# A fused attention and two expert layers: order of the pooled products, one more early place for a weight tile, an even schedule of weight loads

## The chip, the cores and the metric

The kernel runs on one core of one Trainium2 chip, in one launch. The metric is the device time of that launch in microseconds. The core's engines are named as in the profile: PE is TensorE's matmul stream and PEld its loads of the stationary operand, DVE is VectorE, ACT ScalarE, POOL GpSimd, and SP the engine whose queue issues all DMA transfers here.

## The reference

Three stages, all in 32-bit floats. The first is attention over 4 batches, 8 heads, 576 positions and head size 64. It has two branches. The pooled branch averages q, k and v over groups of four positions (144 of them), does full softmax attention and repeats each output row four times. The local branch lets each position see only neighbours at a distance under four:

```
q_d, k_d, v_d = mean over groups of 4;  out_up = repeat(sm_attn(q_d, k_d, v_d), 4)
scores = where(|i - j| < 4, scale * q @ k.T, -1e9)
out = out_up + softmax(scores) @ v          # then (B, H, S, D) -> x of (2304, 512)
```

The second stage is a soft mixture of experts: `logits = x @ phi` (32 slots), a softmax over tokens makes 32 slot inputs, each of 8 experts takes four of them through `relu(s @ w1) @ w2` (512 to 1024 to 512), and a softmax over slots gives each token its mixture. The third is a second mixture with 8 experts over all 2304 tokens, whose gates are normalised eight times over rows and columns in turn; the result is the sum of `P[:, e] * relu(x @ w1[e]) @ w2[e]`.

## The kernel before, in words

**Units and steps.** The attention is cut into 16 units: one batch and one pair of heads each, with the 2 x 64 head columns on 128 partitions. The work on a unit is some 35 small parts (`load_q`, `transpose_k`, `score_pool`, `pool_exp`, `av_pool`, `x_add` and so on, functions of the unit's number). A list written out by hand, `ORDER`, names the parts with a lag; step u of the loop calls part p for unit u - lag. So at any time parts of about seven units are in flight, and every engine executes its instructions in the order in which the list emits them. Step u loads q for unit u + 3 and k for unit u + 4, transposes q of unit u + 2, and does the pooled and local products of unit u - 2. Parts in `BATCH` run once in four steps (the logits of the expert layer and their running softmax). What is left of units 14 and 15 and of the last batch stands in a second list, `TAIL`, with some idle matmuls (`tail_fill`).

**The parts around the change.** `pt` (L549, L554) transposes the normalised pooled probabilities and pools v; `pt_copy` (L562, L566) copies both out of PSUM as `ptd` and `vd`. `av_pool` (L578) multiplies them into `up`: for each of the two heads one product over 128 rows of that head's own block and one over 64 rows of the block that the two heads share, accumulated into that head's 64 output partitions. Before, the order is own and shared of head 0, then own and shared of head 1. In the trace each fp32 matmul is two matmul and two weight-load instructions. `up_copy` (L587) copies `up` to `ups`, of which there are two buffers; `av_loc` (L595) makes the local output `loc`, twelve matmuls with the heads in turn; `x_add` (L605) adds `ups`, repeated four times, to `loc` and writes one of five tiles `xt0` to `xt4` (unit modulo 5). `x_nat` (L628, L629) transposes `xt` for the token layout. `score_pool` (L458) makes the pooled scores `sd` of the next unit in one PSUM buffer, which `pool_exp` (L501) reads.

**Weights of the first expert layer.** Both weight matrices are read as 32 tiles `wa` of 128 x 2048 floats, 8,192 bytes a partition and 1024 KB each (`load_wa`, L311), in the order of `wa_order`. The first 20 have places of their own: `NW` = 4, then `NX` = 7, 4 and 5. The 4 + 7 = 11 exist from the start, on the left of SBUF below the attention's pools. The next 4 lie on the right, where q, k and their transposes were, and exist after the last `score_pool`. The last 5 lie on the left over the attention's pools `ld` (three buffers vw), `st` (two block diagonals), `wk` (work tiles) and `wl` (`xt0` to `xt4` and small ones), in that order of addresses, and are asked for when `TAIL` has been emitted; two further tiles ("late") follow above them. Tiles 23 to 32 reuse the first places as the layer's first products `h` (L877) free them. Loads wait place by place: a tile's transfer waits for the last reader of whatever lies under it, and since one queue issues them, a load behind a waiting one waits too.

`LOADS` says at which step how many weight tiles are asked for (`load_w`); a load of a step stands on SP behind q and k of that step and ahead of v. After the last step all places that exist are filled.

**The first expert layer after the attention.** `h` takes the sixteen tiles of w1, expert by expert (the last two are the late ones, the 21st and 22nd tile), then `so` (L934) the sixteen tiles of w2. Then the second layer begins (`ap`, L992), whose weights w1s and w2s come on the same queue and whose order is planned by due times; the change leaves it alone.

Of the kernel before, what the change touches and what calls it, by code (L numbers as in the profile page):

```python
# [8 lines left out]
FP32 = mybir.dt.float32  # L9
# [31 lines left out]
    ("tail_fill", 2), ("tok_sum", 3), ("tail_fill", 5), ("tok_add", 3),  # L41
]

LOADS = {-2: 1, 2: 1, 4: 1, 6: 1, 8: 1, 10: 1, 12: 1, 13: 1, 14: 1, 15: 2}

PADDED = 2

# [138 lines left out]
def attn_moe_moe_kernel(  # L186
# [23 lines left out]
    SD = S // 4  # L210
# [1 line left out]
    NSET = S // (4 * QB)  # L212

    QS = 1.0 / float(D) ** 0.5 / 16.0
    NW, NX = 4, (7, 4, 5)
    BLK = 256
    NB = N // BLK

# [64 lines left out]
    def load_next(n=1):  # L283
        nonlocal nw
        for _ in range(n):
            if nw < 4 * E:
                load_wa(nw)
                nw += 1
# [29 lines left out]
    with ExitStack() as actx:  # L318
# [5 lines left out]
        wk = actx.enter_context(tc.tile_pool(name="wk", bufs=2))  # L324
# [245 lines left out]
        def av_pool(u):  # L570
            d = U[u]
            up = d["up"] = p1.tile([128, SD], FP32, name="up", tag="t1")
            vd, ptd = d["vd"], d["ptd"]
            for h in range(2):

                for i in (2 * h, 1):
                    ks = slice(64 * h, 64 * h + 64) if i == 1 else slice(0, 128)
                    nc.tensor.matmul(  # L578
                        out=up[64 * h:64 * h + 64, :], lhsT=vd[ks, i, :], rhs=ptd[ks, i, :],
                        start=(i != 1), stop=(i == 1),  # L580
                    )

        def up_copy(u):
            d = U[u]
            up = d["up"]
            ups = d["ups"] = wk.tile([128, 2, SD // 2, 1], FP32, name="ups", tag="ups")
            nc.scalar.activation(out=ups, in_=up.rearrange("p (a g o) -> p a g o", a=2, o=1), func=ACTF.Copy)  # L587

        def av_loc(u):
# [211 lines left out]
        for u in range(-3, nu):  # L801
            for n, lag in ORDER:
                if n == "load_w":
                    load_next(LOADS.get(u, 0))
                elif n not in BATCH:
# [29 lines left out]
    with mctx:  # L835
# [18 lines left out]
        for j in range(KD):  # L854
            nc.tensor.matmul(
                out=sit[:, j].rearrange("p e s -> p (e s)"), lhsT=ssum[:, 128 * j:128 * j + 128], rhs=stack[:, 0, :],
                start=True, stop=True,
# [13 lines left out]
        for e in range(E):  # L871
# [4 lines left out]
            for a, j in order:  # L876
# [3 lines left out]
                    start=(e == 0), stop=(e == E - 1),  # L880
# [36 lines left out]
        for j in range(KF):  # L917
# [3 lines left out]
                start=True, stop=True,  # L921
# [4 lines left out]
        for e in range(E):  # L926
            for j in range(KF):
                g = j % 4
                w = wt[2 * E + 2 * e + j // 4]
                if e >= E - 2 and j % 4 == 0:  # L930
# [5 lines left out]
                    start=(e == 0 and j < 4), stop=(e == E - 1 and j >= 4),  # L936
# [492 lines left out]
```

## Time and profile before

| what | us |
|---|---|
| median of 3 runs (lowest, highest) | 1014.33 (1012.17, 1015.3) |
| profiled execution, its own time | 1014.82 |
| its span, first to last instruction | 1013.1 |
| PE / PEld busy | 979.1 / 900.4 |
| DVE / ACT / POOL busy | 713.5 / 550.6 / 592.9 |

The mean granted clock of TensorE in that execution is 0.997 of 2.4 GHz. The chain of work that ended last has 84% of its time on PE, 5% on ACT, 4% on DVE and 3% on DMA. The 40 slices of the page show DMA busy at 0.9 or more of the time in the first 100 us, about 0.6 to 0.8 in the next 50, again 0.9 in the 50 after that, and little later. Stretches of the span: steps of the attention to about 135 us, `TAIL` to about 163, `h` to 180, `so` to 207, then the second expert layer.

A line of the timeline reads: start, duration, engine, line, operation, out<-in, shape and count, and in brackets the engine's idle time before it with what ended it. A line of the chain reads: start, duration, what the end of the program was waiting for at that time. In the stretches, each engine has its busy time and number of instructions; then follow TensorE's granted clock, the busy share of the DMA engines (over 1 where transfers overlap) and GB/s.

### The profile page before, as it was taken

The page shows a single profiled execution, that of the slowest core. Times are in us where ns is not written, and L with a number is a line of the kernel's source. Part 1 is how long each engine was busy: PE and PEld are TensorE (multiplying, and loading weights), DVE is VectorE, ACT ScalarE, POOL GpSimd, SP SyncE. Part 2 cuts the span into 40 slices and gives each one's busy share as a digit, 9 for nine tenths or more (in the row PEclk, how much of TensorE's full clock was granted, in tenths as well). Part 3 has the DMA queues.
Part 4 walks back from the last instruction along what each step waited for, and adds up shares of the span by engine and source line. Part 5 has one row for each costly group of instructions (what it writes and reads, how often), then busy time and mean ns, then how long its engine had stood idle before and what let it go on. Part 6 is the DMA issues. An engine that isn't in the chain of part 4 may idle for free.

```text
span 1013.1 us, 23034 instructions
## 1 busy us (share of the span) xinstructions
PE 979.1 (97%) x9353; PEld 900.4 (89%) x9353; DVE 713.5 (70%) x1251; ACT 550.6 (54%) x1055; POOL 592.9 (59%) x456
## 2 busy tenths in 40 slices
PE   5999999889999999999999999999999999999998
PEld 4776665469999899989999999999999999999998
DVE  5878862255887767767686768667866776778766
ACT  4666641154566656745565556455655555565453
POOL 6554431033667557855774676576757674776544
PEclk9999999999999999999999999999999999999999
DMA  9999688944002200220031004000400130000111
GB/s 186 211 179 214 166 302 306 387 182 167 1 2 84 84 1 2 87 81 1 2 125 43 1 2 163 5 2 8 160 1 2 42 126 2 2 2 21 64 43 63
DMA packets 96956, 89.11 MB, mean 88 GB/s; under 512 B 65876, under 2 KB 65876, under 8 KB 96852
## 3 DMA queue, kind: packets, MB, share of 16 engines
q1 hardware_dynamic: 96852, 87.65, 29.4%
q8 instruction: 74, 1.21, 0.5%
q14 instruction: 30, 0.25, 0.1%
HBM read 82.92 MB, written 4.72 MB: 87 GB/s over the span
## 4 chain that ended last, share of the span: by engine, by line
PE 84%; ACT 5%; DVE 4%; DMA 3%; issue 2%; POOL 1%; SPq 1%; ACTq 0%; DVEq 0%; POOLq 0%
PE y L1121 63%; PE z L1063 6%; DMA wa<-in_moe_w_dram 3%; PE up L578 2%; PE y L1134 2%; PE ap L992 2%; DVE wt L1053 2%; ACT pd L501 1%; ACT kt L412 1%; PE sd L458 1%; PE knt L368 1%; PE as L1003 1%; DVE acc L1159 1%; PE loc L595 1%; PE sl L445 1%
## 5 line engine op out<-in xcount | busy, mean ns | idle before, releaser
L1121 PE MATMUL y<-wt,ot 128*128 128x256 f32 x5880 | 745.3, 277 | 4.0 <-DVE acc L1159 3.9
L1121 PEld LDWEIGHTS y<-wt,ot 128*128 128x128 f32 x5880 | 715.5, 188 | 18.0 <-issue 16.8
L1100 POOL TENSOR_TENSOR ot<-ft,ot 128x512 fp32r<-128x512 f32 x280 | 366.5, 1332 | 275.3 <-ACT ot L1096 177.8
L1159 DVE SCALAR_TENSOR_TENSOR acc<-y,pg,acc 128x256 f32<-128x256 f32 x315 | 200.5, 637 | 163.0 <-PE y L1121 162.3
L1096 ACT ACTIVATE ot<-ft 128x512 fp32r<-128x512 f32 x280 | 169.6, 627 | 145.8 <-DVE ft L1090 145.5
L1075 ACT ACTIVATE ot<-z 128x512 fp32r<-128x512 f32 x218 | 130.2, 598 | 163.3 <-PE z L1063 124.0
L1090 DVE SCALAR_TENSOR_TENSOR ft<-z,ft 128x512 f32<-128x512 f32 x280 | 189.9, 678 | 2.3 <-ACT ft L1086 2.1
L1063 PE MATMUL z<-c,a4s 128*128 128x256 f32 x576 | 159.0, 277 | 1.0 <-DVE a4s L1008 1.0
L1079 DVE SCALAR_TENSOR_TENSOR ot<-z,ot 128x512 fp32r<-128x512 f32 x218 | 147.8, 679 | 1.4 <-ACT ot L1075 1.2
L1063 PEld LDWEIGHTS z<-c,a4s 128*128 128x128 f32 x576 | 107.9, 188 | 1.5 <-DVE a4s L1008 1.2
L1086 ACT ACTIVATE ft<-z 128x512 f32<-128x512 f32 x140 | 83.1, 594 | 0.0
L516 POOL TENSOR_TENSOR pl<-pl,l 128x384 f32<-128x384 f32 x16 | 13.3, 833 | 62.7 <-DVE l L512 26.1
L1053 POOL TENSOR_TENSOR wt<-w2s,wt 128x1024 fp32r<-128x1024 f32 x17 | 41.7, 2454 | 9.2 <-ACT wt L1046 9.2
L1053 POOL TENSOR_TENSOR wt<-ts,wt 128x1024 fp32r<-128x1024 f32 x15 | 36.2, 2434 | 6.8 <-ACT wt L1046 6.8
L527 DVE STREAM_TRANSPOSE bd<-pl 32x384 f32<-32x384 f32 x64 | 36.4, 569 | 1.4
L1046 ACT ACTIVATE wt<-ts 128x1024 fp32r<-128x1024 f32 x32 | 33.5, 1055 | 4.4 <-PE y L1121 4.4
L1033 POOL TENSOR_TENSOR ts<-w2s 128x1024 f32<-128x1024 f32 x14 | 33.8, 2411 | 0.0
L997 DVE TENSOR_TENSOR aps<-ap,aps 128x512 fp32r<-128x512 f32 x16 | 11.0, 686 | 23.9 <-ACT aps L996 23.9
L412 ACT ACTIVATE kt<-knt 64x576 f32<-64x576 f32 x32 | 20.5, 641 | 12.8 <-DVE kd L401 12.5
L578 PE MATMUL up<-ptd,vd 64*64 64x144 f32 (+1 forms) x128 | 25.9, 310 | 1.5 <-ACT vd L566 1.5
L1046 ACT ACTIVATE wt<-w2s 128x1024 fp32r<-128x1024 f32 x25 | 26.0, 1047 | 0.0
L1053 DVE TENSOR_TENSOR wt<-ts,wt 128x1024 fp32r<-128x1024 f32 x17 | 25.4, 1493 | 0.2 <-ACT wt L1046 0.2
(188 smaller groups left out, 816.8 us busy)
## 6 DMA issues: line engine op xcount, KB each, us to landing
wa<-in_moe_w_dram SPq DMA_DIRECT2D x32, 1024.0 KB, 12.2
w1s<-in_moe_w_dram SPq DMA_DIRECT2D x16, 1024.0 KB, 5.0
w2s<-in_moe_w_dram SPq DMA_DIRECT2D x16, 1024.0 KB, 5.2
vw<-in_v_dram SPq DMA_DIRECT2D x62, 96.0 KB, 4.1
kn<-in_k_dram SPq DMA_DIRECT2D x32, 144.0 KB, 4.7
qn<-in_q_dram SPq DMA_DIRECT2D x32, 144.0 KB, 4.8
out_dram<-acc SPq DMA_DIRECT2D x18, 256.0 KB, 2.0
vw<-in_v_dram SPq DMA_DIRECT2D x2, 88.0 KB, 4.8
```

Source lines behind the costliest of these rows:

```text
L578: nc.tensor.matmul(out=up[64 * h:64 * h + 64, :], lhsT=vd[ks, i, :], rhs=ptd[ks, i, :], start=(i != 1), stop=(i == 1),)
L1046: nc.scalar.activation(out=tt[e, i][:, 0], in_=w_of(e, i), func=ACTF.Copy)
L1053: eng.tensor_tensor(out=t[:, 1], in0=w_of(e, i), in1=t[:, 0].bitcast(FP32), op=ALU.subtract)
L1063: nc.tensor.matmul(out=zt[n, k][:, f, :], lhsT=a4s[e % 2][:, f0:f0 + 128], rhs=c4[:, BLK * b:BLK * b + BLK], start=True, stop=True,)
L1075: nc.scalar.activation(out=t[:, 0], in_=zv(n, i, k), func=ACTF.Relu)
L1079: nc.vector.scalar_tensor_tensor(out=t[:, 1], in0=zv(n, i, k), scalar=0.0, in1=t[:, 0].bitcast(FP32), op0=ALU.max, op1=ALU.subtract)
L1086: nc.scalar.activation(out=t, in_=zv(n, i, k), func=ACTF.Relu)
L1090: nc.vector.scalar_tensor_tensor(out=t, in0=zv(n, i, k), scalar=0.0, in1=ft[n, other], op0=ALU.max, op1=op)
L1096: nc.scalar.activation(out=t[:, 0], in_=ft[n, name], func=ACTF.Copy)
L1100: nc.gpsimd.tensor_tensor(out=t[:, 1], in0=ft[n, name], in1=t[:, 0].bitcast(FP32), op=ALU.subtract)
L1121: nc.tensor.matmul(out=yt[n, bank][:, HD * half:HD * half + HD], lhsT=ot[n, name][:, l, f, :], rhs=tt[e, j][:, r, f, :], start=(m == 0 and ...
L1159: nc.vector.scalar_tensor_tensor(out=o, in0=in_, scalar=pg[:, t, e:e + 1] if e else 1.0, in1=o, op0=ALU.mult, op1=ALU.add)
```

## The change

`av_pool` first does the own products of both heads, then the shared products of both. `NX` becomes (8, 4, 4): twelve places exist from the start and four, not five, come at the end. `ups` has one buffer. `LOADS` asks for twelve tiles instead of eleven, never two in a step.

```
-LOADS = {-2: 1, 2: 1, 4: 1, 6: 1, 8: 1, 10: 1, 12: 1, 13: 1, 14: 1, 15: 2}
+LOADS = {-2: 1, 1: 1, 3: 1, 5: 1, 7: 1, 9: 1, 10: 1, 11: 1, 12: 1, 13: 1, 14: 1, 15: 1}
-    NW, NX = 4, (7, 4, 5)
+    NW, NX = 4, (8, 4, 4)
-            for h in range(2):
-
-                for i in (2 * h, 1):
-                    ks = slice(64 * h, 64 * h + 64) if i == 1 else slice(0, 128)
+
+            for own in (True, False):
+                for h in range(2):
+                    ks, i = (slice(0, 128), 2 * h) if own else (slice(64 * h, 64 * h + 64), 1)
                     nc.tensor.matmul(
                         out=up[64 * h:64 * h + 64, :], lhsT=vd[ks, i, :], rhs=ptd[ks, i, :],
-                        start=(i != 1), stop=(i == 1),
+                        start=own, stop=not own, skip_group_check=True,
                     )
-            ups = d["ups"] = wk.tile([128, 2, SD // 2, 1], FP32, name="ups", tag="ups")
+            ups = d["ups"] = wk.tile([128, 2, SD // 2, 1], FP32, name="ups", tag="ups", bufs=1)
```

## Rows read from the trace of the kernel before

**Rows 1.** The page's first line.

```profile
span 1013.1 us, 23034 instructions
```

**Rows 2.** The chain that ended last, 0 to 380 us.

```profile
by line: PE y L1121 27.7%; DMA wa<-in_moe_w_dram 7.7%; PE up L578 6.2%; PE y L1134 5.9%; PE z L1063 3.5%; ACT pd L501 3.4%; ACT kt L412 3.3%; PE sd L458 2.7%; issue 2.6%; PE knt L368 2.6%; PE loc L595 1.8%; PE sl L445 1.6%; PE ap L992 1.6%;
...
49.63 1.56 PE up L578 x8
...
55.45 0.71 PE sd L458 x8
...
56.81 1.56 PE up L578 x8
...
73.97 1.17 PE sd L458 x8
```

**Rows 3.** Stretches: us, then busy us (count) of PE, PEld, DVE, ACT, POOL; clock, DMA, GB/s.

```profile
49.52:56.69 7.17, 6.76 (x121) 5.28 (x119) 6.30 (x13) 5.36 (x17) 4.10 (x6) 1.00 1.19 218
71.03:78.20 7.17, 6.75 (x98) 4.90 (x98) 5.06 (x11) 2.36 (x8) 4.09 (x5) 0.76 0.76 140
150.00:158.50 8.50, 7.58 (x76) 5.44 (x74) 2.34 (x7) 3.39 (x10) 0.00 (x0) 1.00 0.49 165
180.00:206.00 26.00, 23.29 (x196) 10.72 (x194) 7.78 (x14) 3.55 (x7) 1.88 (x3) 1.00 1.05 386
```

**Rows 4.** Waits of SP's queue, 150 to 160 us: total, times, longest.

```profile
SPq L311 <- PE loc L595: 14.2, 1, 14.2
SPq L311 <- PE xh L629: 7.0, 1, 7.0
```

**Rows 5.** Timeline of the first expert layer, TensorE's weight loads.

```profile
175.91 0.30 PEld L877 LDWEIGHTS h<-wa,slt 128*32 128x32 f32 x4 [0.50 <-DMA wa<-in_moe_w_dram]
178.47 0.16 PEld L877 LDWEIGHTS h<-wa,slt 128*32 128x32 f32 x8 [2.27 <-DMA wa<-in_moe_w_dram]
...
194.75 0.16 PEld L934 LDWEIGHTS so<-wa,hT 128*32 128x32 f32 x8 [0.17 <-issue]
...
198.21 0.13 PEld L934 LDWEIGHTS so<-wa,hT 128*32 128x32 f32 x4 [0.30 <-issue]
200.07 0.16 PEld L934 LDWEIGHTS so<-wa,hT 128*32 128x32 f32 x8 [1.74 <-DMA wa<-in_moe_w_dram]
...
202.78 0.16 PEld L934 LDWEIGHTS so<-wa,hT 128*32 128x32 f32 x8 [1.14 <-DMA wa<-in_moe_w_dram]
```

**Rows 6.** Timeline of a plain turn, TensorE's weight loads.

```profile
92.53 0.19 PEld L578 LDWEIGHTS up<-ptd,vd 128*64 128x64 f32 x2
92.92 0.19 PEld L578 LDWEIGHTS up<-ptd,vd 64*64 64x64 f32 x2 [0.20 <-issue]
...
94.08 1.02 PEld L595 LDWEIGHTS loc<-bd,vw 128*64 128x64 f32 x24 [0.20 <-issue]
95.22 0.42 PEld L628 LDWEIGHTS xn<-ident,xt 128*128 128x128 f32 x4
...
98.39 0.48 PEld L458 LDWEIGHTS sd<-kd,qd 64*72 64x72 f32 x8 [0.53 <-issue]
```

**Rows 7.** Timeline of the same turn, VectorE.

```profile
92.82 0.75 DVE L401 TENSOR_REDUCE kd<-knt 128x144 f32<-128x576 f32 x1
...
95.41 0.76 DVE L605 TENSOR_TENSOR xt<-loc,ups 128x576 f32<-128x576 f32 x1 [0.58 <-PE loc L595]
```

**Rows 8.** Tile qn, 49.2 to 53.4 us: its two transfers of unit 8.

```profile
L351 SPq DMA_DIRECT2D qn<-in_q_dram x2: 402/1892/3381, 49.4 to 49.8; - x2
...
DMA to landing us min/median/max: 7.7/8.1/8.4
```

**Rows 9.** Timeline of TensorE, 59.5 to 61 us.

```profile
60.03 0.66 PE L368 MATMUL qnt<-ident,qn 96*128 96x96 f32 x6
```

**Rows 10.** Timeline of SP's queue, 150 to 152 us.

```profile
151.10 0.37 SPq L311 DMA_DIRECT2D wa<-in_moe_w_dram  x1
```

**Rows 11.** Line L311, all 32 weight tiles of the first expert layer.

```profile
DMA to landing us min/median/max: 5.4/12.2/17.4
```

## The prediction

> **What bounds the kernel now.** I read the profiled execution first: 1014.82 us, of which the span is 1013.1 [rows 1]; the 1.7 around it are taken as unchanged. The median of the three runs, 1014.33, is 0.5 lower, so I sum against 1014.82 and take 0.5 off at the end. The second expert layer (from about 209 us) is one stream of TensorE products and no edit touches it, so the change is worth what it moves before 209.
>
> Next the chain of waits over the first 380 us. The reader is to see two things. In the attention part, one turn of the loop is the distance between two `up` groups, 56.81 - 49.63 = 7.18 us, and TensorE's pooled product stands in it whole with 1.56 us [rows 2]. By its first line `up` has 6.2% of 380 us, 23.6 us, so fifteen of the sixteen units' products lie on the path (23.6 / 1.56). The loop is: `up`, its copy and seven more steps of ScalarE, the score product `sd` 0.71, `knt`, `up`. After the attention the same line gives 7.7%, 29 us, to transfers of weight tiles `wa`.
>
> Third, the table by stretch: the DMA engines are at 0.49 between 150 and 158.5 us, and at 1.05 and 386 GB/s from 180 to 206 [rows 3]; at that rate a tile of 1024 KB takes 2.72 us. Fourth, the waits of SP say why there was a hole: one weight load waits for the local products of the last unit, the next one 7.0 us for `xh`, the last transposes of unit 15 [rows 4]. Last, TensorE's weight loads in the first expert layer show what the hole costs: a load for `h` waits 2.27 us for a tile, and three for `so` 1.74 and twice 1.14; where no tile is waited for the idle time there is 0.30, and 0.17 behind a `cp` [rows 5].
>
> **The change, part by part.**
>
> *The order of the pooled products.* Now each of the four matmuls starts its loads 0.39 us after the one before: 0.19 us of loads, then 0.20 idle [rows 6]; four make 1.55. The shape changes each time (128 rows, 64, 128, 64). Afterwards equal shapes stand in pairs, on different halves of the output. The trace has both kinds of pair. The local products alternate halves with 128 rows: twelve matmuls of 96 columns in 95.22 - 94.08 = 1.14, 0.095 each; times 144/96, the second of a pair adds 0.14. The score products alternate 64-row halves at 144 columns: eight loads in 0.48, so 0.12 a matmul [rows 6]. First pair 0.39 + 0.14, second 0.39 + 0.12: 1.04 instead of 1.55, an estimate of 0.51 saved a unit. Bounds: nothing, if something other than the change of shape makes the idle 0.20; and 0.77, if each pair takes the time of one. A loss I exclude here: same four matmuls, same shapes, fewer changes. I take 0.51 because the nearest rows have the same tiles and operands' sizes.
>
> The Trainium skill bears on both ends. "TensorE: Matmul & The Clock Gate", Part 3 (What overlaps and what doesn't), says that a weight load overlaps a running matmul only where the row groups differ; the first pair has the same rows, so its second would wait, and the saving would be some 0.26. The same part gives a pack the time of one matmul plus about 4 ns a tile, which is the end at 0.77. The trace agrees with neither for 128 rows: 0.095 a matmul is less than one after the other and more than 4 ns.
>
> Does the loop shrink by as much? ScalarE's branch and the `sd` branch both run through `up`, so both lose 0.51. VectorE is next: in a turn it is idle 0.58 us before `xt`, waiting for the local products, which come behind `up` [rows 7]; without that wait its turn is 7.18 - 0.58 = 6.60. The loop goes to 6.67, just above it. Savings over 0.58 would be capped in the plain turns. Fifteen times 0.51 is 7.65.
>
> *One buffer for `ups`.* `up_copy` now waits until `x_add` of the unit before has read it. Behind it on ScalarE are the copies of k and everything of that turn. `x_add` ends at 96.17 [rows 7], more than four us ahead of the next copy; in the tail it runs as soon as the first copy is done and the second copy is behind a whole `pt`. Cost nothing; without that cover it would be at most `x_add`'s 0.76 per turn.
>
> *Weight tiles a step earlier.* Up to step 7 each comes one step earlier, from step 9 on one each step; by step 14 two more than before have been asked for, and the loop's end asks for one less at once. On SP each costs an issue, and 2.72 us of the DMA engines, ahead of the next vw, qn and kn. The engines are already full there (share 1.19 at 49.52 to 56.69) [rows 3]. The tightest is unit 8's q: issued at 49.4 and 49.8, landing 7.7 to 8.4 later, so at 58.2 [rows 8]; its transposes begin at 60.03 [rows 9]. The slack is 1.8, and by then four `up` on the path bring the use forward by 2.0: 0.2 late. I charge 0.6 for this and its neighbours together (0, if SP also gets ahead; 2.7, one tile, if all of one comes in front). The gain of the attention part is then 7.65 - 0.6 = 7.0.
>
> *The twelfth place.* This counts twice. One tile less remains behind the attention part, and the places move. From sizes in the code: the region behind the first weight places holds vw (9,216 bytes a partition), the block diagonals (12,288), the work tiles (16.5 KB, now 576 less), and then xt0, which is unit 15's. Five places of 8,192 end at 40,960 and cover xt0 from 38.3 KB (thousand bytes) on; four end at 32,768 and don't. The second place asked for is the topmost: it is the one that waits for `xh` now, and the three behind it on SP wait with it. Afterwards all four need no more than the local products of unit 15. xt0 falls under the fifth load, which by then finds a queue of four tiles.
>
> So the stream starts at 151.10, less 7.0 [rows 10], with four tiles, instead of one and a hole until 158.5. With 5.4 us from issue to landing [rows 11] and 2.72 a tile, in the old time scale: the sixth tile, the last that `h` needs, lands at 151.1 + 5.4 + 13.6 = 170.1, where `h` without waits wants it at 176; the sixteenth at 197.3, where `so` without waits wants it at 199.9. No tile is late. What goes are the waits of rows 5: 2.2 in `h` (2.27 - 0.30, and 0.50 - 0.25 just before), and in `so` 1.44 + 2 x 0.97 = 3.4. Sum 5.6. What is late next is nothing on DMA: the margin is 2.6 us, and TensorE's products set the pace.
>
> Sum: 7.0 + 5.6 = 12.6; 1014.8 - 12.6 = 1002.2, and 0.5 off for the median: 1001.7 us.
>
> **Rivals.**
> - *The pairs don't overlap* (the skill's rule on row groups does this): 15 x 0.26 = 3.9, less 0.3, plus 5.6: 9.2, 1005 us. For it: TensorE's loads already show an unexplained idle 0.20. Against: the local products.
> - *The pairs overlap fully*: eight plain turns capped at 0.58, seven at 0.77: 10.0 - 0.7 + 5.6 = 14.9, 999.5.
> - *DMA keeps the attention part's pace*: the engines are full in the plain turns, a tile comes ahead of q, and the loop waits for q. If eight turns of fifteen give nothing back: 3.6 + 5.6 = 9.2, 1005. For it: share 1.19 and the slack of 1.8. Against: in the step with logits, 71.03 to 78.20, the share is 0.76, so the engines have room to catch up there [rows 3].
> - *The places don't fall as I work out*, and a load still waits for `xh`: the hole stays, and only one tile less follows: 2.7 instead of 5.6, 1004.5.
> - *Slower, by TensorE's clock.* From 71.03 to 78.20 the granted clock is 0.76 [rows 3]: about half of it at 1.2 GHz, after a logits step with small products and a pause; `sd` took 1.17 there and 0.71 at 2.4 GHz [rows 2]. A dip costs (1 - 0.76) x 7.17 = 1.7 us at most. TensorE will be less busy in every turn; if the clock then falls once in each of fourteen turns, 24 us come on top of the forecast: 1025. It decides from eight such dips on (8 x 1.7 = 13.6). Against: in a plain turn the clock is 1.00 now, with 0.53 us idle ahead of `sd` [rows 3, 6]. [...]
> - *Nothing comes of it*: the idle 0.20 stays, and the stream is bound elsewhere: 1014.
>
> **How the numbers follow.** Forecast 0.54; no overlap 0.13; full overlap 0.10; DMA's pace 0.08; places 0.08; clock 0.05 (of it 0.04 slower than before); nothing 0.02. The forecast's own spread is about 1.5 us to either side (the clock's dips, the three runs' 3 us). The range 997.5 to 1007 leaves out the clock, nothing, and the edges. A difference under 0.3% (3 us) can't be told from none: faster 0.92, same 0.03, slower 0.05.
>
> **What would show it.** `up`'s four pairs of loads begin at intervals with two idle gaps, not four, and span about 1.04. The turn is 6.6 to 6.7, with VectorE's idle before `xt` near 0.05. SP's wait for `xh` is gone or falls on the fifth load of that series; the DMA share has no hole behind the last local products; `h` and `so` show no wait on `wa`. The forecast is wrong if `up` still spans 1.3 or more, if `qnt` waits for DMA by more than 1 us, or if the granted clock falls in plain turns.

## The result and the profile after

The changed kernel takes 1000.07 us (median of 4 runs, 998.03 to 1002.43) beside 1013.78 (4 runs). The ratio is 0.9866, with a 95% interval of 0.9839 to 0.9893: 13.6 us gained, 10.8 to 16.3 (one minus the ratio, times the median before). Forecast were 1001.7 us and 12.6 gained.

The page's first lines, its row of DMA slices, and the chain's shares by engine:

```profile
span 998.0 us, 23050 instructions
PE 967.7 (97%) x9353; PEld 895.0 (90%) x9353; DVE 714.1 (72%) x1251; ACT 550.4 (55%) x1055; POOL 592.4 (59%) x456
...
DMA  9999999940013000400130013001300130000111
...
PE 85%; DVE 8%; ACT 3%; issue 2%; POOL 1%; DMA 0%; SPq 0%; DVEq 0%; POOLq 0%; ACTq 0%
```

The chain no longer has DMA in it (3% before), and VectorE's share has doubled. The stretch of full DMA engines is unbroken now, eight slices or 200 us; before, the slices from 101 to 177 us stood at 6 to 8.

TensorE's weight loads of a plain turn, the counterpart of [rows 6], and below them the matmuls of the same `up`:

```profile
87.72 0.20 PEld L578 LDWEIGHTS up<-ptd,vd 128*64 128x64 f32 x4
88.11 0.20 PEld L578 LDWEIGHTS up<-ptd,vd 64*64 64x64 f32 x4 [0.20 <-issue]
88.50 1.02 PEld L595 LDWEIGHTS loc<-bd,vw 128*64 128x64 f32 x24 [0.20 <-issue]
89.64 0.42 PEld L628 LDWEIGHTS xn<-ident,xt 128*128 128x128 f32 x4
...
87.72 0.86 PE L578 MATMUL up<-ptd,vd 128*64 128x144 f32 x8
```

There are two gaps instead of four, and `up` takes 0.78 (88.50 - 87.72) instead of 1.55. Four loads go out in the 0.20 us that two took: the second matmul of a pair costs 0.01 us.

Stretches of the changed kernel (columns as in [rows 3]): a plain turn; the time from the last local products on; the `so` part.

```profile
81.29:87.72 6.43, 6.06 (x121) 4.93 (x120) 6.10 (x13) 5.36 (x17) 3.25 (x5) 1.00 0.99 205
140.50:149.00 8.50, 7.58 (x68) 5.31 (x64) 2.85 (x9) 3.73 (x10) 0.00 (x0) 1.00 0.91 301
166.00:192.00 26.00, 25.71 (x218) 11.93 (x210) 8.22 (x15) 3.54 (x7) 2.25 (x3) 1.00 1.05 386
```

The hole of 0.49 in [rows 3] is now 0.91, and from 166 to 192 TensorE is busy 25.7 of 26 us (23.3 before in 180 to 206). SP's waits from 138 to 150 us, as in [rows 4], and the issue of the load that waits for `xh`:

```profile
SPq L311 <- PE loc L595: 9.2, 1, 9.2
SPq L311 <- PE xh L629: 4.9, 1, 4.9
...
148.38 0.37 SPq L311 DMA_DIRECT2D wa<-in_moe_w_dram  x1
```

The wait for `xh` is still there, but it is the fifth load of the series that has it: four are issued between 141.0 and 142.5, and the queue is not empty when the fifth follows at 148.4. No weight load of `h` or `so` waits for a tile. What follows `so` is `sop`, its transposes. Their loads before, then in the changed kernel their loads and matmuls, and VectorE ahead of them:

```profile
207.17 0.97 PEld L946 LDWEIGHTS sop<-stack,sos 128*128 128x128 f32 x8 [0.16 <-issue]
...
192.10 0.97 PEld L946 LDWEIGHTS sop<-stack,sos 128*128 128x128 f32 x8 [0.59 <-issue]
192.14 1.05 PE L946 MATMUL sop<-stack,sos 128*128 128x32 f32 x8 [0.43 <-DVE sos L941]
...
190.41 1.13 DVE L905 TENSOR_TENSOR c<-cp,c 32x384 fp32r<-32x384 f32 x2 [0.57 <-ACT c L903]
191.57 0.42 DVE L941 COPY sos<-so 128x256 f32<-128x256 f32 x1
```

A new wait of 0.4 stands in front of `sop`: VectorE, which copies `so` out, is now still at the last `c` pieces.

Where the time came from is read off three starts in each profiled execution: the first `up`, the first `h`, the first `ap`. From `ap` to the end every kernel here takes 804.0 to 804.6 us.

| kernel | first `up` to first `h` | first `h` to first `ap` |
|---|---|---|
| before | 135.6 | 44.9 |
| changed | 125.8 | 39.9 |

So 9.8 us came from the attention and 5.0 from the first expert layer. Of the 9.8, some 1.5 are not the change's. In the kernel before, the turn from 65.0 to 76.2 us took 11.2, with a granted clock of 0.85; its last 3.5 us ran at the lower of TensorE's two levels, 1.2 GHz:

```profile
64.90:76.20 11.30, 10.88 (x136) 8.25 (x134) 7.76 (x16) 6.57 (x20) 5.37 (x7) 0.85 0.85 166
65.00:71.00 6.00, 6.00 (x57) 4.51 (x56) 4.51 (x9) 4.41 (x15) 2.53 (x4) 1.00 0.99 186
71.00:72.70 1.70, 1.28 (x26) 0.99 (x28) 1.66 (x5) 1.31 (x4) 0.00 (x0) 1.00 0.40 86
72.70:76.20 3.50, 3.50 (x66) 2.75 (x58) 1.59 (x5) 0.75 (x2) 2.74 (x3) 0.51 0.82 166
```

Three of the kernels below with the old order of products (the second, fifth and eighth) take 9.65 for it at 1.00, the third again 11.2. The changed execution has a fall of its own, at a cost of about 1.5, in the first turn (7.48, as in the first run; 5.99 in the fourth, seventh, ninth and tenth, which have the new order too), half of it at 1.2 GHz:

```profile
28.00:35.50 7.50, 7.20 (x116) 5.50 (x114) 5.47 (x11) 4.82 (x15) 2.58 (x4) 0.75 1.06 228
```

Such falls come and go between executions of kernels alike in this respect. In this pair the two about cancel.

### The profile page after: what moved, and what is told of

It reads as the page before. It is cut to its first block, busy times and chain, and to the rows that moved or that the text cites. A ratio compares the mean times of both kernels' runs of the same rounds, so it can differ in the third digit from the quotient of the medians.

```text
span 998.0 us, 23050 instructions
## 1 busy us (share of the span) xinstructions
PE 967.7 (97%) x9353; PEld 895.0 (90%) x9353; DVE 714.1 (72%) x1251; ACT 550.4 (55%) x1055; POOL 592.4 (59%) x456
## 4 chain that ended last, share of the span: by engine, by line
PE 85%; DVE 8%; ACT 3%; issue 2%; POOL 1%; DMA 0%; SPq 0%; DVEq 0%; POOLq 0%; ACTq 0%
PE y L1121 64%; PE z L1063 6%; PE y L1134 2%; PE ap L992 2%; DVE bd L527 2%; DVE wt L1053 2%; PE h L877 1%; PE so L934 1%; PE as L1003 1%; DVE acc L1159 1%; PE loc L595 1%; DVE kd L401 1%; PE up L578 1%; PE knt L368 1%; PE sd L458 1%
## 5 line engine op out<-in xcount | busy, mean ns | idle before, releaser
L1121 PE MATMUL y<-wt,ot 128*128 128x256 f32 x5880 | 745.3, 277 | 4.0 <-DVE acc L1159 4.0
L412 ACT ACTIVATE kt<-knt 64x576 f32<-64x576 f32 x32 | 20.6, 642 | 12.9 <-DVE kd L401 12.6
L1134 PE MATMUL y<-wt,ot 128*128 128x256 f32 x192 | 24.9, 278 | 0.0
```

The lines of the kernel that those rows point to most:

```text
L1121: nc.tensor.matmul(out=yt[n, bank][:, HD * half:HD * half + HD], lhsT=ot[n, name][:, l, f, :], rhs=tt[e, j][:, r, f, :], start=(m == 0 and ...
```

## The experiments

Theory: the order of the products shortens the attention, the places shorten the first expert layer, and the two add. Rivals stand in the expectations. "Gained" is against the kernel before on the same chip, by the ratio.

**1. The order alone**: the edit of `av_pool` as in the change, all else as before.

> The kernel before with the new order of the pooled products alone. My theory (order and places give separate gains that add): `up` takes 0.79 us a unit as in the changed kernel, the plain turn goes from 7.17 to about 6.45, the first `h` product comes 9 to 10 us earlier, but the hole ahead of the load that waits for `xh` stays, and with it the waits for `wa` in `h` (2.2) and `so` (3.4): 9 to 10 us gained, about 1004. Rival (the stream of weights ends the first layer at a time of its own, so a faster attention is taken back by the waits for tiles): the waits in `h` and `so` grow by what the attention gains, and less than 4 us remain, above 1009.

1004.84 us beside 1015.07; ratio 0.9895 (0.9869 to 0.9921), 10.7 gained. First `up` to first `h` 125.8, the same as in the changed kernel; `h` to `ap` 45.1, the same as before. TensorE's waits (total, times, longest), in the kernel before from 163 to 225 us, then here from 150 to 206:

```profile
PEld so L934 <- DMA wa<-in_moe_w_dram: 4.5, 5, 1.7
PEld h L877 <- DMA wa<-in_moe_w_dram: 2.8, 2, 2.3
...
PEld so L934 <- DMA wa<-in_moe_w_dram: 4.2, 4, 1.7
PEld h L877 <- DMA wa<-in_moe_w_dram: 3.1, 2, 2.4
```

The waits for tiles hardly change: the full stream of weights starts at `xh`, so it moves forward with the attention. The rival falls.

**2. The places, one `ups` buffer and the schedule, with the old order**:

```
-    NW, NX = 4, (7, 4, 5)
+    NW, NX = 4, (8, 4, 4)      # with the new LOADS, and bufs=1 for ups
```

> The kernel before with the places (8, 4, 4), one buffer for `ups` and the new schedule of loads; the old order of products. My theory (the region behind the early places no longer covers xt0, so no load waits for `xh`): the hole is gone, `h` and `so` no longer wait for tiles, 5 us gained, about 1009, and the attention part keeps its turn of 7.17. Rival (what counts is the one tile fewer in the late stream): 2.7 us gained, 1011, and a load of the first four late ones still waits for `xh`.

1010.14 beside 1015.07; ratio 0.9947 (0.9929 to 0.9965), 5.4 gained. `h` to `ap` takes 39.9, to `h` 134.0 with the old turn of 7.17. No wait for `wa` in `h` or `so`. The theory stands: by the traces some 9 to 10 us for the order and 5 for the places. (By the times 10.7 and 5.4 make 16.1, more than the 13.6 of both together; but their intervals are 2.6 and 1.8 to either side, too wide to count this against the sum.)

**3. Four late places in place of five, eleven early ones kept**:

```
-    NW, NX = 4, (7, 4, 5)
+    NW, NX = 4, (7, 4, 4)
```

> The kernel before with four late places in place of five and the eleven early ones kept, so one place fewer in all, nothing else changed. My theory (where the places lie is what counts): the load that lies over xt0 is now the fifth of its series, four go out with the last local products, 4 to 5.5 us gained, about 1009, with the same number of tiles left to load as before. Rival (the twelfth early place is what counts): no gain, 1013 to 1015, since no tile more is loaded during the attention.

1011.31 beside 1015.07; ratio 0.9961 (0.9944 to 0.9979), 4.0 gained, with one place *fewer* than before. `h` to `ap` 40.9. From 150 to 206 us `h` waits for no tile, and `so` for less:

```profile
PEld so L934 <- DMA wa<-in_moe_w_dram: 2.1, 4, 1.1
PE so L934 <- DMA wa<-in_moe_w_dram: 1.3, 2, 0.9
```

SP's wait for `xh` (5.0) falls on the fifth load of the series here too. By the traces, four of the five us come from what lies under the places. The last one goes with the twelfth early place: the second run has it and takes 39.9, and so does the seventh, under the old schedule.

**4. The changed kernel without VectorE's L511**:

```
-            nc.vector.tensor_scalar(out=l, in0=l, scalar1=EPS, scalar2=None, op0=ALU.add)
```

> The changed kernel without the VectorE instruction L511 of each unit, which adds 1e-9 to sums of exponentials (left out; each sum is at least 1). My theory (VectorE's own instructions now set the plain turn): the turn of 6.45 gets 0.2 shorter, some 8 to 12 turns feel it, 1.5 to 2.5 us gained against the changed kernel, about 998. Rival (the loop through `up`, ScalarE and `sd` still sets the turn, or the transfers of q do): turn unchanged, within 0.5 us of the changed kernel.

999.9; ratio to before 0.9847 (0.9819 to 0.9875), where the changed kernel has 0.9866 and 0.9865. These intervals are too wide to tell the theory's 2 us from none, so the traces must decide. To `h` 124.0, beside 125.8 and, in the tenth run, 124.7. Turns of the same place: 6.42 in the changed kernel, 6.43 here; 7.77 and 7.53 in the next. The chain of the changed kernel from 76 to 96 us goes through VectorE:

```profile
81.46 0.70 DVE kd L401
...
83.45 0.76 DVE xt L605
...
88.13 0.66 DVE kd L401
```

The same chain here goes through `up`, ScalarE and `sd`, as before the change:

```profile
81.50 0.81 PE up L577 x8
...
86.56 0.71 PE sd L458 x8
...
87.92 0.81 PE up L577 x8
```

My theory was wrong by its size. VectorE's turn is 6.67 (from one `kd` to the next, 81.46 to 88.13) and the loop's 6.42, so VectorE is the longer of the two, but by 0.25. As I read it, the turn right after one with logits doesn't feel this, since TensorE takes 8.4 there and VectorE catches up; the next one does. Taking 0.24 from VectorE gives the path back to the old loop at once. Something else took a part too: in this trace the transposes `qnt` wait for their q twice, 1.6 us in all, where the changed kernel's execution has no such wait behind the first `up`.

**5 and 6. What makes the idle 0.20 us**: two looks at the order and the shape. The sixth sums rows that the reference leaves out, so it is a look at the engine alone.

```
+            for n, (own, h) in enumerate(((True, 0), (False, 1), (True, 1), (False, 0))):   # fifth
-                    ks = slice(64 * h, 64 * h + 64) if i == 1 else slice(0, 128)
+                    ks = slice(0, 128)                                                       # sixth
```

> The kernel before with the four products ordered own head 0, shared head 1, own head 1, shared head 0: output halves alternate, but the shape (128 rows, 64 rows) still changes each time. If the idle 0.20 us comes with a change of shape: four gaps stay and `up` keeps 1.55 us. If it comes from accumulating on the same half right away: the gaps go, `up` falls to 0.8 to 1.1.

> The kernel before in its old order with all four products over 128 rows (the shared block is then summed over both heads' rows, so the pooled values differ from the reference). If the idle 0.20 us comes with a change of shape: no gaps between the four, `up` about 1.0 to 1.2, as the same half follows itself; one shape change fewer ahead of `loc` too. If it comes from accumulating on the same half: gaps stay and `up` keeps about 1.55.

One run each: 1013.97 and 1003.2. TensorE's loads in the fifth, halves in turn and shapes mixed:

```profile
84.05 0.19 PEld L577 LDWEIGHTS up<-ptd,vd 128*64 128x64 f32 x2
84.44 0.19 PEld L577 LDWEIGHTS up<-ptd,vd 64*64 64x64 f32 x2 [0.20 <-issue]
84.82 0.19 PEld L577 LDWEIGHTS up<-ptd,vd 128*64 128x64 f32 x2 [0.20 <-issue]
```

and in the sixth, old order and one shape, loads and then matmuls:

```profile
80.45 0.45 PEld L578 LDWEIGHTS up<-ptd,vd 128*64 128x64 f32 x8
80.87 1.10 PEld L595 LDWEIGHTS loc<-bd,vw 128*64 128x64 f32 x24
...
80.45 0.72 PE L578 MATMUL up<-ptd,vd 128*64 128x144 f32 x8
80.99 1.17 PE L595 MATMUL loc<-bd,vw 128*64 128x96 f32 x24
```

The gap belongs to the change between 128 and 64 rows. Alternating halves without equal shapes gains nothing (1.55); equal shapes without alternating take 0.54 from the first matmul of `up` to the first of `loc` (80.45 to 80.99), with no gap even ahead of `loc`. What the change bought is two changes of shape fewer.

It is not any change of the number of rows. Later in the same turn of the changed kernel, loads go from 128 rows to 96, to 72 and back to 128 without such a gap:

```profile
83.61 0.14 PEld L629 LDWEIGHTS xh<-ident,xt 128*128 128x128 f32 x1
83.73 0.57 PEld L368 LDWEIGHTS qnt<-ident,qn 96*128 96x128 f32 x6
84.33 0.45 PEld L549 LDWEIGHTS ptp<-ident,pd 72*128 72x128 f32 x6
84.85 0.16 PEld L554 LDWEIGHTS ptp<-vw,fours 128*32 128x32 f32 x8
```

**7. The changed kernel with the old schedule**:

```
-LOADS = {-2: 1, 1: 1, 3: 1, 5: 1, 7: 1, 9: 1, 10: 1, 11: 1, 12: 1, 13: 1, 14: 1, 15: 1}
+LOADS = {-2: 1, 2: 1, 4: 1, 6: 1, 8: 1, 10: 1, 12: 1, 13: 1, 14: 1, 15: 3}
```

> The changed kernel with the old schedule of weight loads (steps 2, 4, 6, 8, 10, 12, 13, 14) and three at step 15. My theory (the schedule is worth little, as all twelve tiles land before the late stream begins or queue behind each other just the same): within 1 us of the changed kernel; the stream at step 15 has seven tiles, so the late four land up to 3 us later, which the margin of 2.6 in `so` nearly covers. Rival (one a step is needed, since the DMA engines are full): 2.7 us or more slower.

999.25; ratio 0.9846 (0.9826 to 0.9866). `h` to `ap` 39.9, no wait for a tile. The schedule is worth nothing that can be told. Its trace takes 126.0 to `h`, with two pauses of TensorE in the middle of `sl`, 3.5 us in all, that the profile puts down to nothing ("issue"); the fourth run's has one of 1.6. What makes them isn't shown.

**8. The kernel before without L511**, the control of the fourth.

> The kernel before without VectorE's L511 (the added 1e-9 left out, as above): the control. My theory (before, the loop through `up` set the turn and VectorE had 0.58 us to spare): turn unchanged at 7.17, less than 0.7 us gained. Rival (VectorE bound the attention before as well): 1.5 to 2.5 us gained.

1015.15 beside 1014.94; ratio 0.9999 (0.9986 to 1.0013), turn 7.17. VectorE did not set the turn before.

**9. The order and four late places, nothing else**: the edits of 1 and 3 together.

> The kernel before with the new order of products and four late places in place of five; the old schedule, eleven early places and two buffers for `ups` stay. My theory (order 9.5 us and places 5, of which the place of xt0 gives 4 and the twelfth early place the last 1): 13 to 14 us gained, 1001 to 1002, some 1 us behind the changed kernel, with short waits of `so` for the last tiles and none of `h`. Rival (with the faster attention the early place counts for more, a whole tile): 2.7 us or more behind the changed kernel.

**10. The changed kernel again**, no edit.

> The changed kernel itself, on the same chip as the run beside it: the yardstick for one us. Order and places add: 14 to 15 us under the kernel before, near 1000. If they don't add (one takes from the other): under 12.

The ninth: 999.89 beside 1014.6; ratio 0.9862 (0.9847 to 0.9877), 14.0 gained. The tenth: 1000.16; 0.9865 (0.9849 to 0.9882), 13.7. So two of the four edits give the whole gain within what can be told; the trace of the ninth has `h` to `ap` at 40.8, the 1 us of the third run. Its profiled execution (1002.12, the slowest of its four) has something else, a turn of 10.0 us. TensorE's transposes of unit 8's q, and that tile's transfers:

```profile
60.78 0.69 PE L368 MATMUL qnt<-ident,qn 96*128 96x96 f32 x6 [2.81 <-DVE l L510]
```

```profile
L351 SPq DMA_DIRECT2D qn<-in_q_dram x2: 402/1972/3542, 50.8 to 51.2; - x2
...
DMA to landing us min/median/max: 7.3/8.4/9.4
```

The wait is put down to VectorE; but the second transfer, issued at 51.2, lands 9.4 later at 60.6, just ahead of 60.78. This is the unit that the prediction named as the tightest. That VectorE's `l` has nothing to do with it is my reading from the times; no run took the transfer away. The tenth trace, of the changed kernel, has two such waits that the profile does put down to the transfers of q (34 to 135 us: total, times, longest), the longer one of unit 7:

```profile
PE qnt L368 <- DMA qn<-in_q_dram: 1.5, 2, 1.0
```

Order and places add: by the traces 134.0 - 124.7 = 9.3 (second and tenth run, whose long logits turn is not slowed) and 5.0 make 14.3. The tenth run measured 13.7 by its ratio, 14.4 by its medians.

## Why the prediction was right, step by step

*The sum.* 12.6 us were forecast and 13.6 measured (13.7 in the repeat). The two parts were 7.0 and 5.6; they are 9.3 and 5.0. That the number came out so near is in part luck: the attention was sized too small, the expert layer a little too large.

*`up`.* Mis-sized: 0.51 saved by the sum, 0.77 measured, the upper bound. The step that failed is "the second of a pair adds 0.14" and 0.12. I took a cadence from `loc` and `sd`, where matmul follows matmul, and added it to a single matmul whose 0.39 is mostly the change of shape (0.135 a matmul without one, sixth run). In a pair the second runs beside the first inside that time. I had weighed two rules of the Trainium skill ("TensorE: Matmul & The Clock Gate", Part 3). By the one, a pack takes the time of one matmul and some 4 ns a tile; the trace agrees, 0.39 a pair as for one before. By the other, a weight load overlaps a running matmul only where the row groups differ; the trace does not agree: four loads on the same 128 rows went out in 0.20 us from 87.72 on, while the first matmul, begun at 87.72, ran.

*The cap by VectorE.* Right in kind, 6.60 forecast and 6.67 measured, but not a cap on every plain turn. Between the traces of the second and the tenth run, eleven of the sixteen units save 0.71 to 0.77, turns right behind one with logits among them; the third and the ninth turn save 0.55, and the second, fourth and thirteenth nearly nothing; in the fourth of the tenth run `qnt` waits 1.0 for q. The rival "full overlap" priced the two together: 999.5. Its mechanism is the nearest to what happened, and its time is nearer than the forecast's 1001.7.

*One `ups` buffer.* Nothing, as forecast: to `h` 125.8 with one buffer and with two (first run).

*The schedule.* The 0.6 charged can't be seen; the seventh run has the old schedule and no gain or loss. The risk behind the charge is real under both schedules: 2.8 us in the ninth run's profiled execution under the old one (by my reading), 1.0 and 0.5 in the tenth's under the new one. Only the 1.0 stands in a turn that saves nothing. So the rival "DMA keeps the attention part's pace" came true in one turn of that execution, not in eight; the sign that the forecast set for being wrong, `qnt` behind DMA by more than 1 us, was about reached there.

*The places.* Right in mechanism: xt0 and the fifth load. `h` gave 2.35 (2.2 forecast), `so` 3.1 (3.4), and 0.4 was given back ahead of `sop`. What I had wrong is the weight of "this counts twice": nearly all is the lie of the places, and the tile loaded earlier gives about 1.

*The clock.* The slower rival, a fall in each of fourteen turns, didn't come. Every trace has one stretch at 1.2 GHz, somewhere between 19 and 33 us; in the changed execution it reaches into the first turn, a plain one, and costs some 1.5 us there, so this sign of being wrong was met once, and in no later turn. The kernel before and the third run have a second fall at 72 to 76 us. Ahead of it the rows above show TensorE busy for all of 65 to 71 us and idle for 0.42 of the next 1.70; what makes the clock fall in some executions and not in others, no run here shows.

## What to carry to other kernels

Keep small matmuls over 64 rows together, and those over 128: here each group between two such changes took the same 0.39 us whether it was one matmul or two. When a load is late, ask what lies under its place and which load stands behind it on the queue: one fewer place, ending below a tile that is read last, gained four of the five us that a richer layout gained (by the traces). A wait taken out of a loop is worth its length only up to the next engine's turn, so price that turn first.

## What the runs showed of the hardware that I had not expected

The pair: two matmuls of equal shape on different output halves take 0.39 us, as one does. And the sixth run: with one shape, four accumulating matmuls take 0.54 us in an order that keeps to one half for two matmuls, 0.135 each; so it isn't the alternation that makes them quick. And the 0.20 us of idle comes with a change between 128 and 64 rows, while changes among 128, 96 and 72 rows in the same turn show none.
